# Gate cells, query prefetch, split loads and warm-up matmuls in a fused attention and MoE kernel

## The chip, the cores and the metric

The kernel runs on one core of a Trainium2 chip. A core has five engines that run side by side and meet through semaphores: PE (TensorE, matrix multiplication; PEld is its weight load), ACT (ScalarE, activation functions), DVE (VectorE, elementwise work), POOL (GpSimd, here for memsets and for issuing loads that cast) and SP (SyncE, here for issuing other transfers). The metric is the device time of one execution in microseconds (us). The kernel before took 968.65 us, the median of 11 runs (965.88 to 978.82).

## The reference

Four images of 384 by 32 pixels with 128 channels are attended. Keys and values are the same: the pixels averaged over 4 by 4 blocks (768 per image) and multiplied by `w_sr`. The attention's output is the input of a two-layer feed-forward net.

```python
kv_pool = kv.reshape(B, H // r, r, W // r, r, C).mean(axis=(2, 4))   # r = 4
kv_flat = kv_pool.reshape(B, -1, C) @ w_sr                           # keys and values
s = (1.0 / np.sqrt(C)) * (q @ kv_flat.transpose(0, 2, 1))
a = softmax(s)                                                       # over the 768 keys
x = (a @ kv_flat).reshape(B * N, C)                                  # 49152 rows
h = x @ w_in                                                         # d_ff = 2048
out = (h * sigmoid(1.702 * h)) @ w_out
```

## The kernel before

The 49152 query rows are cut into 96 groups of 512 (index i for attention, g for the feed-forward net, here called MoE), and four groups make a supergroup (index s, 24 of them). Keys of an image come in six chunks of 128 (index jc). The work has two halves of 48 groups: attention, then MoE, then attention, then MoE.

**Fills and drains.** A fill takes up to three (group, chunk) pairs: PE multiplies into half of six score banks of PSUM, and one activation of ScalarE (exponential in `fill_attn`, L324; gelu in `fill_moe`, L490) moves up to 128x1536 numbers to SBUF, to the tile `ag`. Fills alternate between two halves of three banks, so a fill p needs the activation of fill p - 2 to have ended. A drain multiplies what is in `ag` by the values (`drain_attn`, L333) or by `w_out` (`drain_moe`, L495), into two other banks, from which DVE evacuates. A planner written in Python, with its own running time `now`, its costs `COST` and its list `extras` of side jobs, decides at build time how PE's instructions of drains and side jobs stand between fills. Each engine then executes its instructions in that order.

**The start.** The keys of image 0 come from raw pixels that GpSimd loads in six chunks (`load_chunk`, L125); PE pools them with a small matrix (`pool_chunk`, L134), DVE copies the result to SBUF (L137), PE makes keys and values (`key_and_value`, L155 and L156) and DVE copies these (L157, L158). The first four supergroups of queries are loaded by GpSimd (L213) and transposed by PE (`transpose_q`, L224, copied out by DVE in L230). The table `first` (L567) gives the order in which this stands around the first 20 fills: ahead of fill 7 the transposes of group 7, ahead of fill 8 the pooling of chunk 2, and so on. `warm` (L276) puts matmuls whose result nobody reads among them.

**Pixels of image 1** are loaded the same way, and written over x tiles that are not yet in use, from group 13 on; from group 16 on PE pools a chunk per group and makes its keys a group later. Images 2 and 3 are added up by accumulating loads during the first MoE stage.

**Later queries** are cast to bf16 in DRAM by GpSimd (`cast_q`, L201), and from there loaded transposed by SP (`load_qT`, L206) into tiles of `qpool`.

**Gates.** `background(i)` runs when the planner reaches group i and issues such loads. GpSimd has little else to do and would issue everything at once; so ahead of a load stands `gate()` (L416 to L419): DVE writes the cell tile `gate_tile`, then GpSimd writes the same cells. The framework that sets the semaphores sees two writers of one place, so GpSimd waits until DVE has come as far as its write. The next gate writes the same cells again.

SP's queue is in order, too: the loads of queries, the writebacks of x (`put_away`, L405), the transposed reloads of x (`bring_back`, L411) and the output stores (L506).

Of the kernel before, what the change touches and what calls it, by code (L numbers as in the profile page):

```python
# [24 lines left out]
def kernel(  # L25
    ctx, tc, q, kv, w_sr, moe_w_in, moe_w_out, out,
):
    nc = tc.nc
# [5 lines left out]
    JC = J // 128  # L34
# [6 lines left out]
    NS = NG // 4  # L41
# [24 lines left out]
    kvsum = ctx.enter_context(tc.tile_pool(name="kvsum", bufs=1))  # L66
    kvres = ctx.enter_context(tc.tile_pool(name="kvres", bufs=2))
    kvtmp = ctx.enter_context(tc.tile_pool(name="kvtmp", bufs=1))
    qpool = ctx.enter_context(tc.tile_pool(name="qpool", bufs=3))
    agpool = ctx.enter_context(tc.tile_pool(name="ag", bufs=1))  # L70
    npool = ctx.enter_context(tc.tile_pool(name="norm", bufs=3))
    opool = ctx.enter_context(tc.tile_pool(name="op", bufs=3))
# [48 lines left out]
    def load_chunk(b, jc):  # L121

        a, ch = divmod(jc, HC)
        t = x_tile(XS - 1 - jc)
        nc.gpsimd.dma_start(out=t, in_=kv_r[b, a, ch])  # L125
        kv_tiles[b, jc] = t.rearrange("p (wp w1 c) -> p w1 wp c", w1=r, c=C)
# [34 lines left out]
    def add_kv(b, n):  # L161
        i, w = divmod(n, r)
        if n == 0:
            kv_sums[b] = kvsum.tile([Hp, 2, Wp, C], F32, name="kvs")
        for i2 in range(2):
            nc.gpsimd.dma_start(out=kv_sums[b][:, i2], in_=kv_p[b, i, w, :, i2],  # L166
                                **({"accum_op": ADD} if n else {}))
# [31 lines left out]
    def cast_q(s):  # L199
        sl = slice(s * SG, (s + 1) * SG)  # L200
        nc.gpsimd.dma_start(out=q_bf[sl, :].rearrange("(p i) c -> p (i c)", p=128),  # L201
                            in_=q_flat[sl, :].rearrange("(p i) c -> p (i c)", p=128))

    def load_qT(s):
        qTs[s] = qpool.tile([128, 1, SG], BF, name="qT")
        nc.sync.dma_start_transpose(out=qTs[s], in_=q_bf[s * SG:(s + 1) * SG, :])  # L206


    QS = 4
# [99 lines left out]
    early = range(NG // R, NG // R + EARLY)  # L309
# [92 lines left out]
    def put_away(n, m):  # L402
        o = m * PART
        lo = n * XS * SG + o * T
        nc.sync.dma_start(out=x_bf[lo:lo + PART * T, :].rearrange("(k p) c -> p k c", p=T),  # L405
                          in_=x[:, o * T:(o + PART) * T].rearrange("p (k c) -> p k c", k=PART))

    def bring_back(n, m):
        o = m * PART
        lo = n * XS * SG + o * T  # L410
        nc.sync.dma_start_transpose(out=x[:, o * T:(o + PART) * T].unsqueeze(1), in_=x_bf[lo:lo + PART * T, :])  # L411

    av_of = {}
    gate_tile = cpool.tile([1, 8], F32)

    def gate():  # L416

        nc.vector.memset(gate_tile, 0.0)  # L418
        nc.gpsimd.memset(gate_tile, 0.0)  # L419

    CAST = 5

    def background(i):

        s = i // 4
        if i % 4 == 0:
            if QS <= s + 2 < NS:
                load_qT(s + 2)
            if CAST <= s + CAST < NS:
                gate()  # L430
                cast_q(s + CAST)
        if i == 13:
            gate()
            for jc in range(JC):
                load_chunk(1, jc)
        if 0 <= i - 17 < JC:
            extras.append((key_and_value, 1, i - 17))
        if 0 <= i - 16 < JC:
            extras.append((pool_chunk, 1, i - 16))
        if i in (30, 34, 38):  # L440
            put_away(0, (i - 30) // 4)
        if i in (33, 37, 41):
            bring_back(0, (i - 33) // 4)
        if i == 26:
            gate()
            nc.gpsimd.dma_start(out=w_in_sb, in_=moe_w_in)
        if i == 34:
            gate()
            nc.gpsimd.dma_start(out=w_out_sb, in_=moe_w_out.rearrange("(o p) c -> p o c", p=128))

    def background_moe(g):

        n, g = divmod(g, 4 * XS)
        m, odd = divmod(g - 9, 2)
        m += FIRST
        if n == 0 and FIRST <= m < RT // PART:
            (bring_back if odd else put_away)(n, m)
        g += n * 4 * XS
        nonlocal low
        if g == 12:  # L460
            low = EARLY * JC
            order[:] = [f for f in order if f >= low // K]
        if g in (40, 46):
            i = early[0] + 4 * (g // 46)
            begun.add(("a", i))
            background(i)
        for b, lo in ((2, 2), (3, 24)):
            if lo <= g < lo + 8:
                gate()
                add_kv(b, g - lo)  # L470
            if g in (lo + 10, lo + 12):
                use_kv(b, (g - lo - 10) // 2)

    def use_kv(b, a):
        nonlocal extra_at
        sum_kv(b, a)
        on_dve(3.5)
        extra_at = max(extra_at, dve + 1.5)
        extras.extend([(transpose_pooled, b, a), (make_k, b, a), (make_v, b, a)])

    extras = []
# [59 lines left out]
    begun = set()  # L541
# [4 lines left out]
    def prepare(p):  # L546

        nonlocal now
        for f, *args in first.get(p, ()):
            if f in COST:  # L550
                now = max(now, free[next_acc()])
            f(*args)
            if f in COST:
                now += COST[f][0]
                free[last_acc] = now + COST[f][1]
        kind, part = seq[p]
        for i, jc in part:
            if (kind, i) not in begun:
                begun.add((kind, i))
                (background if kind == "a" else background_moe)(i)  # L560
            while kind == "a" and ((key_and_value, i // GB, jc) in extras or (transpose_q, i) in extras):
                f, *args = extras.pop(0)
                now = max(now, free[next_acc()]) + COST[f][0]
                f(*args)
                free[last_acc] = now + COST[f][1]

    first = {  # L567
        0: [(pool_chunk, 0, 0), (transpose_q, 0), (warm, 1), (key_chunk, 0, 0), (transpose_q, 1), (warm, 1)],
        1: [(value_chunk, 0, 0), (warm, 3)],
        2: [(pool_chunk, 0, 1), (warm, 2), (key_and_value, 0, 1), (warm, 1), (transpose_q, 2)],  # L570
        3: [(transpose_q, 3)],
        4: [(transpose_q, 4)],
# [52 lines left out]
    for n in range(len(seq)):  # L625
        fill(n + 2)
        while True:
# [33 lines left out]
            kind, i, c = source[0]  # L661
# [55 lines left out]
```

## Time and profile before

The profiled execution took 965.16 us, its span 963.4 us.

| engine | busy us | what it does most |
|---|---|---|
| ACT | 944.1 | 512 gelu activations (688.4 us), 189 exponentials (250.0 us) |
| PE | 949.0 | four groups of matmuls: L488 414.7, L495 413.7, L333 162.2, L322 151.1 us |
| DVE | 337.9 | evacuations and a share of the exponentials |
| POOL | 68.3 | issues of loads, 38 gates |

A line of the timeline has the start, the busy time, the engine, the source line, the operation, what it writes and reads with sizes, the count, and in brackets the idle time of the engine ahead of it with the engine that ended it. A row can merge several instructions of the same kind. PE's matmuls overlap and their ends are modelled, so its busy time is above the time in which it is needed.

### The profile page before, as it was taken

Reading aid. Unit: us, or ns where it says so; the run is one execution under the profiler, and the core shown is the slowest. Engines: PE = TensorE matmul, PEld = TensorE weight load, DVE = VectorE, ACT = ScalarE, POOL = GpSimd, SP = SyncE. Lnnn points to the kernel's source line nnn. Section 1 sums busy time; section 2 is a strip of 40 time slices with the busy share of each in tenths; the row PEclk is TensorE's granted clock in tenths of the full one; section 3 lists DMA queues with packets and bytes.
Section 4 is the critical chain, followed back from the end, with each engine's and each line's share of the span. In section 5 each row is a group of like instructions: output and inputs, shape, how many; then the busy total and the mean of one; then the engine's idle time right before and its main releaser. Section 6 shows DMA issues by size and latency. Waiting matters only on the chain.

```text
span 963.4 us, 15072 instructions
## 1 busy us (share of the span) xinstructions
PE 949.0 (99%) x6285; PEld 501.6 (52%) x6285; DVE 337.9 (35%) x721; ACT 944.1 (98%) x706; POOL 68.3 (7%) x117
## 2 busy tenths in 40 slices
PE   7899999999999999999999999999999999999997
PEld 3577777444444444444446777744444444444443
DVE  4444333111577877777613333310110101010010
ACT  4999999999999999999999999999999999999997
POOL 4020100330000332000000000000000000000000
PEclk9999999999999999999999999999999999999999
DMA  9799993999852799215449795472222222222222
GB/s 183 149 203 157 167 198 77 126 156 181 166 110 39 107 143 122 35 30 81 62 73 171 127 205 115 106 127 38 44 34 44 42 34 40 38 33 38 39 35 43
DMA packets 372804, 94.38 MB, mean 98 GB/s; under 512 B 346688, under 2 KB 370368, under 8 KB 372416
## 3 DMA queue, kind: packets, MB, share of 16 engines
q1 hardware_dynamic: 342512, 60.78, 37.3%
q0 software_dynamic: 29168, 32.51, 22.7%
q8 instruction: 49, 0.80, 0.4%
q10 hardware_dynamic: 1056, 0.13, 0.1%
q14 instruction: 19, 0.16, 0.1%
HBM read 52.49 MB, written 48.23 MB: 105 GB/s over the span
## 4 chain that ended last, share of the span: by engine, by line
ACT 93%; PE 5%; issue 1%; DMA 1%; DVE 0%; POOL 0%; POOLq 0%
ACT ag L490 71%; ACT ag L324 21%; PE banks L322 3%; PE banks L333 2%; DMA x<-in_q_dram 1%; PE banks L134 0%; ACT L490 0%; PE banks L224 0%; PE banks L276 0%; DVE qT L230 0%; ACT L324 0%; DVE x L345 0%; PE banks L495 0%; DVE o_sb L503 0%; POOL x L125 0%
## 5 line engine op out<-in xcount | busy, mean ns | idle before, releaser
L490 ACT ACTIVATE ag<-banks 128x1536 bf16<-128x1536 f32 x512 | 688.4, 1561 | 0.0
L488 PE MATMUL banks<-x,w_in_sb 128*128 128x512 bf16 x1536 | 414.7, 379 | 0.2
L495 PE MATMUL banks<-ag,w_out_sb 128*128 128x512 bf16 x1536 | 413.7, 379 | 0.5 <-ACT ag L490 0.5
L324 ACT ACTIVATE ag<-banks 128x1536 bf16<-128x1536 f32 (+2 forms) x189 | 250.0, 1444 | 6.6 <-PE banks L322 6.4
L495 PEld LDWEIGHTS <-w_out_sb 128*128 128x128 bf16 x1536 | 149.8, 98 | 180.4 <-issue 1.0
L488 PEld LDWEIGHTS <-w_in_sb 128*128 128x128 bf16 x1536 | 148.2, 98 | 179.0 <-issue 22.2
L503 DVE STREAM_TRANSPOSE o_sb<-banks 128x512 f32<-128x512 f32 x96 | 68.7, 716 | 398.8 <-PE banks L495 386.3
L333 PEld LDWEIGHTS <-ag 128*128 128x128 bf16 x2304 | 145.7, 98 | 42.8 <-issue 0.7
L333 PE MATMUL banks<-v,ag 128*128 128x129 bf16 x2304 | 162.2, 220 | 0.3 <-DVE v L158 0.3
L322 PE MATMUL banks<-qT,kT 128*128 128x512 bf16 x552 | 151.1, 381 | 5.9 <-ACT ag L324 3.3
L345 DVE TENSOR_TENSOR x<-banks,rec 128x384 bf16<-128x384 f32 x128 | 71.3, 557 | 4.4
L342 DVE RECIPROCAL rec<-banks 128x3 f32<-128x3 f32 x128 | 23.0, 180 | 138.0 <-PE banks L333 137.9
L390 DVE SCALAR_TENSOR_TENSOR ea<-ea,eb 128x512 f32<-128x512 f32 x96 | 65.9, 686 | 2.7
L322 PEld LDWEIGHTS <-kT 128*128 128x128 bf16 x552 | 47.3, 98 | 33.5 <-issue 5.8
L166 POOL DMA_DIRECT2D kvs<-in_kv_dram x32 | 40.6, 1319 | 30.9 <-DMA kvs<-in_kv_dram 28.6
L419 POOL MEMSET gate_tile<- 1x8 f32 x38 | 4.9, 129 | 434.6 <-DVE gate_tile L418 434.6
L379 DVE TENSOR_SCALAR ea<-banks 128x512 f32<-128x512 f32 x24 | 16.6, 691 | 28.0 <-PE banks L363 28.0
L392 DVE SCALAR_TENSOR_TENSOR ag<-ea,ee 128x512 bf16<-128x512 f32 x24 | 16.6, 691 | 0.8
L385 DVE SCALAR_TENSOR_TENSOR eb<-eb,ea 128x512 f32<-128x512 f32 x24 | 16.4, 685 | 0.7
L230 DVE COPY qT<-banks 128x512 bf16<-128x512 bf16 x15 | 10.2, 690 | 7.8 <-PE banks L224 7.8
L387 DVE TENSOR_SCALAR ea<-eb 128x512 f32<-128x512 f32 x24 | 10.6, 442 | 0.7
L201 POOL DMA_DIRECT2D q_bf<-in_q_dram x20 | 9.9, 496 | 7.6 <-DMA x<-in_kv_dram 6.1
(58 smaller groups left out, 126.7 us busy)
## 6 DMA issues: line engine op xcount, KB each, us to landing
out_dram<-o_sb SPq DMA_DIRECT2D x382, 64.0 KB, 2.0
x_bf<-x SPq DMA_DIRECT2D x16, 768.0 KB, 5.9
kvs<-in_kv_dram POOLq DMA_DIRECT2D x32, 384.0 KB, 6.7
q_bf<-in_q_dram POOLq DMA_DIRECT2D x20, 512.0 KB, 7.4
x<-in_kv_dram POOLq DMA_DIRECT2D x12, 512.0 KB, 12.1
x<-in_q_dram POOLq DMA_DIRECT2D x7, 256.0 KB, 15.2
w_in_sb<-in_moe_w_in_dram POOLq DMA_DIRECT2D x1, 512.0 KB, 5.3
w_out_sb<-in_moe_w_out_dram POOLq DMA_DIRECT2D x1, 512.0 KB, 10.9
```

What stands on the lines that cost most here:

```text
L166: nc.gpsimd.dma_start(out=kv_sums[b][:, i2], in_=kv_p[b, i, w, :, i2], **({"accum_op": ADD} if n else {}))
L322: nc.tensor.matmul(ps[:, k, :], kTs[i // GB][:, jc * 128:(jc + 1) * 128], rhs, start=True, stop=True)
L324: nc.scalar.activation(place([("a",) + c for c in chunks]), ps, AF.Exp, scale=scale)
L333: nc.tensor.matmul(av_of[u][:, k * (C + 1):(k + 1) * (C + 1)], weights(("a", i, jc))[:, o:o + T], vs[i // GB][:, jc, 0:C + 1], start=(jc = ...
L342: nc.vector.reciprocal(rec, ps[:, :, C])
L345: nc.vector.tensor_tensor(to, ps[:, :, 0:C], rec.unsqueeze(2).broadcast_to([128, TS, C]), MUL)
L379: nc.vector.tensor_scalar(a, ps, scale / LN2, -126.0, MUL, MAX)
L390: nc.vector.scalar_tensor_tensor(a, a, COEFFS[k], b, ADD, MUL)
L488: nc.tensor.matmul(ps[:, k, :], w_in_sb[:, fc * 128:(fc + 1) * 128], x[:, g % (4 * XS) * G:(g % (4 * XS) + 1) * G], start=True, stop=True)
L490: nc.scalar.activation(place([("m",) + c for c in chunks]), ps, AF.Gelu_apprx_sigmoid)
L495: nc.tensor.matmul(o_of[g], w_out_sb[:, fc, :], weights(("m", g, fc)), start=(fc == 0), stop=(fc == FCH - 1))
L503: nc.vector.transpose(o_sb, o_of.pop(g))
```

## The change

- A gate writes one of eight cells in turn, instead of all eight.
- `qpool` has four buffers instead of three, and transposed queries are loaded three supergroups ahead of the running one instead of two.
- The six loads of image 1's pixels are issued in two parts of three, at groups 10 and 13, each behind a gate. Its chunks are pooled one group sooner, from group 15 on, and the keys from group 16 on.
- In the first MoE stage, the background of group 48 alone is run ahead, at g = 40. That of group 52 is run when the second attention half reaches it.
- Of the warm-up matmuls in `first`, three are gone.

```diff
-    qpool = ctx.enter_context(tc.tile_pool(name="qpool", bufs=3))
+    qpool = ctx.enter_context(tc.tile_pool(name="qpool", bufs=4))
...
+    gates = [0]
+
     def gate():
 
-        nc.vector.memset(gate_tile, 0.0)
-        nc.gpsimd.memset(gate_tile, 0.0)
+        one = gate_tile[:, gates[0] % 8:gates[0] % 8 + 1]
+        gates[0] += 1
+        nc.vector.memset(one, 0.0)
+        nc.gpsimd.memset(one, 0.0)
...
         if i % 4 == 0:
-            if QS <= s + 2 < NS:
-                load_qT(s + 2)
+            if QS <= s + 3 < NS:
+                load_qT(s + 3)
...
-        if i == 13:
+        if i in (10, 13):
             gate()
-            for jc in range(JC):
+            for jc in range(i - 10, i - 7):
                 load_chunk(1, jc)
-        if 0 <= i - 17 < JC:
-            extras.append((key_and_value, 1, i - 17))
         if 0 <= i - 16 < JC:
-            extras.append((pool_chunk, 1, i - 16))
+            extras.append((key_and_value, 1, i - 16))
+        if 0 <= i - 15 < JC:
+            extras.append((pool_chunk, 1, i - 15))
...
-        if g in (40, 46):
-            i = early[0] + 4 * (g // 46)
-            begun.add(("a", i))
-            background(i)
+        if g == 40:
+            background(early[0])
...
-        0: [(pool_chunk, 0, 0), (transpose_q, 0), (warm, 1), (key_chunk, 0, 0), (transpose_q, 1), (warm, 1)],
-        1: [(value_chunk, 0, 0), (warm, 3)],
+        0: [(pool_chunk, 0, 0), (transpose_q, 0), (warm, 1), (key_chunk, 0, 0), (transpose_q, 1)],
+        1: [(value_chunk, 0, 0), (warm, 1)],
```

## The prediction

> **What bounds the kernel now.** I read the page's busy table first, then ScalarE's own waits, then its timeline at the start, then what DVE and GpSimd did in the same microseconds.
>
> ```profile
> span 963.4 us, 15072 instructions
> PE 949.0 (99%) x6285; PEld 501.6 (52%) x6285; DVE 337.9 (35%) x721; ACT 944.1 (98%) x706; POOL 68.3 (7%) x117
> ACT 93%; PE 5%; issue 1%; DMA 1%; DVE 0%; POOL 0%; POOLq 0%
> ```
>
> ScalarE (ACT) is busy for 944.1 of 963.4 us and carries 93% of the chain that ended last. PE shows 99%, but matmul ends are modelled; only 5% of the chain is PE's. None of ScalarE's 702 activations and copies, nor its four table loads, is touched by the diff. So the change can only move ScalarE's idle time: 963.4 - 944.1 = 19.3 us. Where that lies is in ScalarE's timeline of the first 160 us (the last column is idle time ahead, and what ended it):
>
> ```profile
> 7.91 0.58 ACT L228 COPY qT<-banks 128x512 bf16<-128x512 bf16 x1 [5.88 <-PE banks L224]
> 9.61 0.60 ACT L324 ACTIVATE ag<-banks 128x512 bf16<-128x512 f32 x1 [1.11 <-PE banks L322]
> 10.74 0.60 ACT L324 ACTIVATE ag<-banks 128x512 bf16<-128x512 f32 x1 [0.53 <-PE banks L322]
> 13.06 4.73 ACT L324 ACTIVATE ag<-banks 128x1024 bf16<-128x1024 f32 x5 [1.72 <-PE banks L322]
> 19.43 1.02 ACT L324 ACTIVATE ag<-banks 128x1024 bf16<-128x1024 f32 x1 [1.65 <-PE banks L322]
> 20.71 1.02 ACT L324 ACTIVATE ag<-banks 128x1024 bf16<-128x1024 f32 x1 [0.26 <-PE banks L322]
> 22.56 55.67 ACT L324 ACTIVATE ag<-banks 128x1536 bf16<-128x1536 f32 x42 [0.82 <-PE banks L322]
> 78.57 67.70 ACT L324 ACTIVATE ag<-banks 128x1536 bf16<-128x1536 f32 x50 [0.34 <-PE banks L322]
> ```
>
> About 10 us lie ahead of 13.06 (with 0.75 before the first table load), 2.73 between 17.79 and 22.56, 0.5 between 22.56 and 78.57, and the last 6.0 us are the drain after the final activation at 957.4. After 78.57 ScalarE never waits: the second half of attention and both MoE stages have nothing to give. Only 2.73 us are near the edited lines. Why does ScalarE wait there? DVE's timeline in that stretch:
>
> ```profile
> 14.24 1.44 DVE L230 COPY qT<-banks 128x512 bf16<-128x512 bf16 x2 [0.27 <-PE banks L224]
> 17.80 0.68 DVE L230 COPY qT<-banks 128x512 bf16<-128x512 bf16 x1 [2.13 <-PE banks L224]
> 17.81 0.07 DVE L418 MEMSET gate_tile<- 1x8 f32 x1
> ```
>
> and GpSimd's (POOL):
>
> ```profile
> 14.68 0.70 POOL L213 DMA_DIRECT2D x<-in_q_dram  x1 [0.57 <-DMA x<-in_q_dram]
> 17.15 0.52 POOL L201 DMA_DIRECT2D q_bf<-in_q_dram  x1 [1.77 <-DMA x<-in_kv_dram]
> 17.66 0.09 POOL L419 MEMSET gate_tile<- 1x8 f32 x1
> ```
>
> DVE sat idle for 2.13 us before copying query group 6 out of PSUM. The profile blames PE's transpose, but PE started that at 15.52 for 0.39 us, so it had long been done. In program order the second gate's DVE memset stands directly ahead of this copy; in the program before it waits for GpSimd, since it overwrites the cell that GpSimd's memset of the first gate writes. GpSimd reached that memset at 17.66, after a cast that itself waited for a landing load. DVE starts within 0.1 us of its end. So a pacing gate, meant to hold GpSimd, held DVE, then PE (matmuls of group 6 at 18.54), then ScalarE. A second cost rides on it: of three stretches of the trace, the granted clock is below 1.00 in the middle one alone.
>
> ```profile
> 13.06:17.80 4.74, 3.39 (x28) 1.92 (x25) 2.30 (x4) 4.73 (x5) 2.02 (x4) 1.00 1.11 216
> 17.80:22.56 4.76, 3.63 (x33) 1.76 (x34) 2.06 (x6) 2.05 (x2) 0.59 (x2) 0.64 1.12 213
> 22.56:36.00 13.44, 10.10 (x106) 5.75 (x102) 5.13 (x14) 13.44 (x11) 0.49 (x1) 1.00 1.08 213
> ```
>
> The columns are length, busy time of PE, PEld, DVE, ACT and POOL, granted clock, DMA share, GB/s. PE idles for 1.7 us, then runs at a mean clock of 0.64, which produces the waits of 0.26 and part of 0.82.
>
> **What the Trainium skill says.** "TensorE: Matmul & The Clock Gate", section "Architectural detail", says that ScalarE's and DVE's queues are strict first-in-first-out: a waiting memset holds every later copy. The trace agrees: 2.13 us. The same page, "What's actually happening", puts PE's clock at half after an idle window of some 3.4 us, and back at full after a busy one. The trace agrees in kind, not in size: 1.7 us of idle sufficed here, and about 4.7 us passed before full speed. "DMA: Bandwidth & Descriptors", section "Issuing engines are not separate DMA queues", says that loads issued by SP and GpSimd share the same 16 engines; the DMA share of 1.08 to 1.14 above, with both queues active from 36 us on, fits.
>
> **The change part by part.**
>
> *Gates in eight cells.* The memsets stay (38 on each engine, one more after; 65 and 94 ns); in the built program the DVE one waits for nothing at first use, while GpSimd's still waits for its own gate's DVE memset. Follow the fills of the score banks (p7 is query group 6, p8 group 7, p9 to p11 pooled chunk 2). Before, ScalarE began p7, p8, p9 and p10 at 19.43, 20.71, 22.56 and 23.90 (22.56 + 1.34). After:
> - group 6's copy starts 0.44 after its transpose (as 12.19 to 12.63): 15.52 + 0.44 = 15.96, and ends at 16.64. Group 7: 16.44 + 0.44 = 16.88 to 17.56.
> - p7's matmuls need the bank that ScalarE leaves at 13.06 + 4 x 0.946 = 16.84, so they run at 16.9 to 17.4; p7 is ready before p6 ends at 17.79. Wait 1.65 becomes 0; p8 follows at 18.74, wait 0.26 becomes 0.
> - chunk 2's pooling: its load had landed by 17.15 (the cast that reuses its semaphore was issued then), so it starts at 17.4; copy to SBUF at +0.59, done +0.88 = 18.3; key matmul 18.4; key copy +0.31 to +0.60 = 19.0; p9's three matmuls to ScalarE 0.85 (77.72 to 78.57): p9 at 19.9.
> - what is late next: chunk 3. It had landed only by 20.26 (the next cast's issue). Pooling 20.3, p10's matmuls 0.40 later, ScalarE 0.85 later: p10 at 21.55, against p9's end at 21.24.
> Gain at p10: 23.90 - 21.55 = 2.35 us. Chunk 4 landed by 22.67 and is then wanted at 23.7, so it holds nothing. Chunk 5 is wanted at 29.52 - 2.35 = 27.2; the landings at 17.1, 20.2 and 22.6 with half a chunk of queries between put it near 26.5, an estimate; if it is late the gain falls by some tenths. Ends: 1.5 (chunks late) to 2.73 (all three waits gone). I take 2.35.
>
> *Three warm-up matmuls fewer* (0.21 us each by their start spacing, 0.64 in all, between 8.9 and 10.3). They bring the first two activations forward by some 0.2 and 0.5 us, but 13.06 follows from pooling chunk 1 at 10.62, which waited for its load (landed by 10.86, next issue). Worth 0. Hidden only while PE keeps its clock. If it drops to half near 12 us, each step of two score matmuls and four transposes costs 2 x 0.43 + 4 x 0.11 = 1.3 us against ScalarE's 0.946, over four steps 1.4 us lost. Bounds 0 and -1.4; I take 0, since 13 stay at the start and five between 7.8 and 12.1.
>
> *Queries three supergroups ahead, four buffers.* In the built program the load of supergroup 4 gets a fresh buffer, so SP may issue it when its cast has landed, about 32.4 (SP's wait for it was 31.2 us from 1.2), not at 35.75; each later one comes some 10.7 us (four groups at 2 x 1.337) sooner. No ScalarE wait in the trace names a query load, so 0 gained. SP stands first in line for the same buffer release as before, so the writebacks and out stores queued behind it are not later. In the MoE stage one load of two moves to the start of the second attention half; with ScalarE idle 0.03 us there, 0.
>
> *Second pixels in two parts, one group sooner.* Three loads leave two groups (2 x 2.67 us) ahead of the gate at 48.42, minus 2.35: 40.7. Pooling begins one group earlier: 58.97 - 2.67 - 2.35 = 53.9. So they have 13 us; before, the first had under 7.9 (51.26 to 58.97) and PE did not wait. The same 96 pooling matmuls and twelve small ones are moved, none added. In 36 to 79 us PE is busy 42.47 of 43.00, so placement may change the two ScalarE waits of 0.13 and 0.34: between -0.5 and +0.7, I take 0. One gate more: 0.16 us on engines with room.
>
> **Sum.** -2.35 + 0 + 0 + 0 = -2.35 us on the profiled execution's 965.16 (span 963.4, 1.8 around it): 962.8. The eleven plain times have a median of 968.65, 3.5 above it; the same subtraction there gives 966.3 us, -0.24%. Half a per cent, 4.84 us, is about what a measurement of this kernel can tell from no change.
>
> **Rivals.**
> - *More than the gate's own stall.* Plain executions take 3.5 us more than the profiled one. If that is late loads at the start, lengthening GpSimd's way to its gate with DVE held meanwhile, the edit returns both: 968.65 - 5.85 = 962.8, faster by 0.6%. For: the spread of 965.9 to 978.8. Against: late loads also delay the pooling, which no gate causes.
> - *The clock drops for want of warm-up.* 966.3 + 1.4 = 967.7. For: one 1.7 us gap was enough. Against: the gaps opened here are about 0.2 to 0.5 us.
> - *The change doesn't do what it says*: DVE was held by something the records miss (a few matmul records can be missing), or chunks 2 to 4 take the wait over. Then 968.6. Against: the 0.1 us between GpSimd's memset and DVE's.
> - *Slower: second pixels not landed.* PE works in order, so pooling at 53.9 stops the score matmuls where it has almost no slack. Two full banks cover 2.7 us. It eats the gain when a load takes 13.2 + 2.7 + 2.35 = 18.2 us, and costs 0.5% at 23: 973.5 or more. For: landing medians of 12.1 and 15.2 us on the page for the first loads, and the query transposes now sharing this stretch. Against: DMA share 0.66 in 40 to 60.
>
> **How the numbers follow.** Forecast 0.62 (its own range 965.3 to 967.6), more than the stall 0.15, clock 0.10, no effect 0.06, slower 0.07. Faster by over 0.5%: 0.16; within: 0.77 (0.62 + 0.10 + 0.06, rounded with the first rival); slower: 0.07. The range 962.5 to 969.4 takes in all but the slower case and the tail of the first rival.
>
> **What would show it.** Right: no idle of 1.65 before an activation near 17.8, DVE copying group 6 near 16 us, clock 1.00 from 17.8 to 22.6, ScalarE's long run starting near 19.9 to 21.6, ScalarE idle of about 17 us in all. Wrong: pooling that waits for a load near 54 us; a clock under 1 between 10 and 16 us; an idle ScalarE anywhere after 80 us; the last activation ending elsewhere than near 955.

## The result, and the profile after

The changed kernel took 963.32 us in the median (12 executions, from 962.83), the kernel before 969.68 (47 executions); the ratio is 0.9932, 95% interval 0.9899 to 0.9965. A second comparison on one chip gave 963.14 against 966.36, ratio 0.9951 (0.9929 to 0.9974). The forecast was 966.3 us, -0.24%. Its full range, 962.5 to 969.4, holds the result, the range of its main case, 965.3 to 967.6, does not; and the gain is two to three times as large, so part of its source was not in my sum.

The ratios here and below leave out executions more than 1.5% above the fastest of their kernel, four of these 12 and five of the 47; with them the mean is 973.4 us against 971.2, so it is the usual execution that became faster, while a faster average is not shown.

The profile on record is of one of those four, 1000.31 us. A second profiled execution of the changed kernel took 962.96 us. Its page, and ScalarE's timeline at the start:

```profile
span 961.1 us, 14956 instructions
PE 940.6 (98%) x6168; PEld 500.8 (52%) x6282; DVE 338.4 (35%) x722; ACT 944.0 (98%) x706; POOL 68.1 (7%) x118
...
9.01 0.60 ACT L324 ACTIVATE ag<-banks 128x512 bf16<-128x512 f32 x1 [0.69 <-PE banks L322]
10.03 0.60 ACT L324 ACTIVATE ag<-banks 128x512 bf16<-128x512 f32 x1 [0.42 <-PE banks L322]
12.87 6.57 ACT L324 ACTIVATE ag<-banks 128x1024 bf16<-128x1024 f32 x7 [2.25 <-PE banks L224]
19.62 1.45 ACT L324 ACTIVATE ag<-banks 128x1536 bf16<-128x1536 f32 x1 [0.18 <-PE banks L322]
21.81 121.98 ACT L324 ACTIVATE ag<-banks 128x1536 bf16<-128x1536 f32 x91 [0.73 <-PE banks L322]
```

Five two-bank activations, followed by two that waited, have become one run of seven. ScalarE's idle time is 961.1 - 944.0 = 17.1 us (19.3 before). DVE's timeline shows why, and the windows the clock (the columns as before):

```profile
15.43 0.06 DVE L422 MEMSET gate_tile<- 1x1 f32 x1
15.76 0.69 DVE L230 COPY qT<-banks 128x512 bf16<-128x512 bf16 x1 [0.27 <-PE banks L224]
16.68 0.69 DVE L230 COPY qT<-banks 128x512 bf16<-128x512 bf16 x1 [0.22 <-PE banks L224]
```

```profile
13.06:17.80 4.74, 4.26 (x43) 2.76 (x44) 3.54 (x8) 4.74 (x6) 2.01 (x4) 1.00 1.11 217
17.80:22.56 4.76, 3.11 (x29) 1.42 (x29) 1.52 (x6) 3.84 (x4) 0.58 (x2) 1.00 1.10 209
```

The gate's memset waits for nothing; ahead of group 6's copy DVE is idle for 0.27 us, not 2.13.

The execution of 1000.31 us has the same start (copies at 15.94 and 16.85, the first three-bank activation at 19.80). What it adds is in ScalarE's timeline, and in PE's:

```profile
19.80 35.41 ACT L324 ACTIVATE ag<-banks 128x1536 bf16<-128x1536 f32 x27 [0.18 <-PE banks L322]
82.22 1.45 ACT L324 ACTIVATE ag<-banks 128x1536 bf16<-128x1536 f32 x1 [27.01 <-PE banks L322]
84.44 9.74 ACT L324 ACTIVATE ag<-banks 128x1536 bf16<-128x1536 f32 x7 [0.78 <-PE banks L322]
103.27 1.45 ACT L324 ACTIVATE ag<-banks 128x1536 bf16<-128x1536 f32 x1 [9.09 <-PE banks L322]
```

```profile
52.91 0.81 PE L322 MATMUL banks<-qT,kT 128*128 128x512 bf16 x3
79.97 0.61 PE L134 MATMUL banks<-sum,x 128*128 128x32 bf16 x16 [26.25 <-DMA x<-in_kv_dram]
```

PE reached the pooling of image 1 at 53.7 and stood still for its first chunk until 79.97: the mechanism and the place of my slower rival. What PE waited for before ScalarE's second long wait, ahead of 103.27, the profile does not name.

### The profile page after: what moved, and what is told of

It is laid out like the page before. It is cut to its first block, busy times and chain, and to the rows that moved or that the text cites. A ratio compares the mean times of both kernels' runs of the same rounds, so it can differ in the third digit from the quotient of the medians.

```text
span 998.4 us, 15070 instructions
## 1 busy us (share of the span) xinstructions
PE 950.8 (95%) x6282; PEld 502.8 (50%) x6282; DVE 338.3 (34%) x722; ACT 944.3 (95%) x706; POOL 68.1 (7%) x118
## 4 chain that ended last, share of the span: by engine, by line
ACT 60%; PE 32%; DMA 5%; issue 2%; DVE 0%; POOL 0%; POOLq 0%
ACT ag L492 51%; PE banks L497 9%; ACT ag L324 9%; PE banks L490 9%; PE banks L333 7%; PE banks L322 7%; DMA x<-in_kv_dram 5%; PE banks L134 0%; ACT L492 0%; PE banks L363 0%; POOL x L213 0%; PE banks L276 0%; DVE o_sb L505 0%; DVE qT L230 0%; POOL x L125 0%
## 5 line engine op out<-in xcount | busy, mean ns | idle before, releaser
L423 POOL MEMSET gate_tile<- 1x1 f32 x39 | 4.8, 123 | 468.3 <-DVE gate_tile L422 468.3
L134 PE MATMUL banks<-sum,x 128*128 128x32 bf16 x192 | 6.8, 179 | 27.4 <-DMA x<-in_kv_dram 27.4
L134 PEld LDWEIGHTS <-x 128*128 128x128 bf16 x192 | 6.5, 98 | 31.4 <-DMA x<-in_kv_dram 29.0
L137 DVE CAST pTc<-banks 128x128 bf16<-128x128 f32 x12 | 3.5, 291 | 39.7 <-PE banks L134 39.7
```

## The experiments

The comparisons were made on three chips, each kernel with the kernel before on its own chip. "Long" below counts the executions above 966 us among all of a kernel.

| kernel | median, its before | ratio (95%) | long | long, its before |
|---|---|---|---|---|
| changed, second comparison | 963.14, 966.36 | 0.9951 (0.9929-0.9974) | 4 of 22 | 28 of 53 |
| changed, two ahead again | 978.29, 966.36 | 1.0048 (1.0011-1.0085) | 14 of 16 | 28 of 53 |
| changed, loads together again | 963.28, 966.36 | 0.9967 (0.9950-0.9985) | 2 of 22 | 28 of 53 |
| before + gates | 968.87, 969.12 | 0.9971 (0.9943-1.0000) | 15 of 22 | 27 of 43 |
| before + three ahead | 964.46, 969.12 | 0.9949 (0.9926-0.9972) | 4 of 22 | 27 of 43 |
| before - casts 8 to 11 | 964.50, 968.62 | 0.9948 (0.9925-0.9970) | 2 of 20 | 51 of 61 |
| before - image 1's loads | 964.77, 968.62 | 0.9941 (0.9916-0.9966) | 2 of 20 | 51 of 61 |
| loads at group 8 | 968.33, 968.62 | 0.9972 (0.9947-0.9998) | 15 of 22 | 51 of 61 |
| loads together, repeated | 964.09, 968.62 | 0.9946 (0.9897-0.9996) | 5 of 12 | 51 of 61 |

The kernel before has its shortest executions at 964 to 965 us, but half or more of all lie above 966, up to 977 and beyond. My forecast rested on one execution of 965.16.

**The changed kernel again** (no edit).

> The changed kernel once more, to see what its usual execution looks like beside the one already profiled, in which PE waited 26 us for image 1's first chunk. If the gates alone made the gain, as forecast: ScalarE's idle time near 17 us, the span near 961, and no wait after 22.6 us. If the loads of image 1 are the cost to be watched: in some executions PE stops at pooling near 54 us for 10 us or more, and these take 985 us or more.

Measured: idle 17.1 us, span 961.1, and no wait longer than 0.22 us after 22.6, as the gates' share of the forecast has it. Eighteen of 22 executions lie between 962.9 and 963.4, one at 967.9, three at 990.8 to 993.6. Both halves of the expectation hold.

**Two supergroups ahead again.**

```diff
-    qpool = ctx.enter_context(tc.tile_pool(name="qpool", bufs=4))
+    qpool = ctx.enter_context(tc.tile_pool(name="qpool", bufs=3))
...
-            if QS <= s + 3 < NS:
-                load_qT(s + 3)
+            if QS <= s + 2 < NS:
+                load_qT(s + 2)
...
-        if g == 40:
-            background(early[0])
+        if g in (40, 46):
+            i = early[0] + 4 * (g // 46)
+            begun.add(("a", i))
+            background(i)
```

> The changed kernel with queries loaded two supergroups ahead from three buffers again, as before; gates, split loads and fewer warm-ups stay. Theory A (the long wait for image 1's chunk comes from a transposed query load that now runs in the same microseconds as image 1's loads): the wait is gone in every execution, all near 963. Theory B (the wait comes from issuing image 1's loads at group 10 and pooling them a group sooner): executions of 985 us and more are as frequent as in the changed kernel, about one in three.

Both theories fail. No execution is near 963 (the shortest took 965.14), and none of 16 reaches 985. PE's waits in the profiled one (981.74 us) name another tensor:

```profile
PE banks L322 <- DMA qT<-q_bf: 15.9, 2, 13.3
PE banks L322 <- ACT ag L324: 3.2, 6, 1.0
PE banks L134 <- DMA x<-in_kv_dram: 2.5, 4, 1.1
```

(total, times, longest.) PE waits 13.3 us at once for transposed queries. With two ahead it is the query load that comes late, and more often than in the kernel before (14 of 16 long, against 28 of 53). Whether the gates or the split loads make it so was not separated.

**Image 1's loads together again.**

```diff
-        if i in (10, 13):
+        if i == 13:
             gate()
-            for jc in range(i - 10, i - 7):
+            for jc in range(JC):
                 load_chunk(1, jc)
-        if 0 <= i - 16 < JC:
-            extras.append((key_and_value, 1, i - 16))
-        if 0 <= i - 15 < JC:
-            extras.append((pool_chunk, 1, i - 15))
+        if 0 <= i - 17 < JC:
+            extras.append((key_and_value, 1, i - 17))
+        if 0 <= i - 16 < JC:
+            extras.append((pool_chunk, 1, i - 16))
```

> The changed kernel with image 1's six loads issued together at group 13 and pooled from group 16 again; gates, three supergroups ahead and fewer warm-ups stay. Theory A: the loads still meet a query transpose, so executions of 985 us stay or become more frequent. Theory B: they are gone, all near 963 to 966. If the gain beyond 2.35 us came from the earlier loads, the fastest executions stay near 963 but the middle of the times moves up by some 3 us, as in the kernel before.

The usual time is unchanged, 963.28: the split of the loads gives nothing in it. The profiled execution (979.48 us) still has PE wait 14.6 us for image 1's chunk, so that wait can come without the split. Neither theory fits in full: no execution reaches 985, but two are long. The repeat:

> Once more the changed kernel with image 1's loads together at group 13, pooled from group 16; two of its 22 executions took more than 964 us, against four of 22 of the changed kernel. If that is a real difference: at most three of this run's lie above 966, and the usual time is 963.2 again. If it was chance: four to eight.

Five of 12 above 966, up to 987.67: by its own terms the low count of the first time was chance. Over both, 7 of 34 are long, against 8 of 34 of the changed kernel; above 980 us lie 1 and 7 (two more of the loads together at 979.5 and 979.8). Whether the split makes the long wait longer stays open.

**The kernel before, three more profiled executions.** Theory C, put in full with the gates below: what the changed kernel gained beyond the start comes from queries that no longer arrive late.

> The kernel before, a second look. Its times reach from 964 to 986 us. If the start alone varies (my first rival): ScalarE's idle time between 13 and 23 us is longer than 2.73 us by what the execution is longer than 965. If image 1's loads vary: ScalarE waits between 55 and 80 us by that much. If neither: 965 us and the waits of the first look.

The first, 965.27 us, shows the waits already known ("neither").

> The kernel before once more, for an execution above 967 us if it comes. Theory C: by what it is above 965, PE waits for a transposed query load (qT) between 55 and 110 us. Rivals: it waits for image 1's chunks there, or the start up to 23 us is longer.

> As the look before it: theory C says that whatever the execution takes above 965 us is PE waiting for qT between 55 and 110 us; the rivals say image 1's chunks, or the start.

These came at 973.94 and 975.52 us. In the first of the two, PE, then ScalarE:

```profile
78.40 0.84 PE L333 MATMUL banks<-v,ag 128*128 128x129 bf16 x12
86.59 1.46 PE L322 MATMUL banks<-qT,kT 128*128 128x512 bf16 x3 [7.34 <-DMA qT<-q_bf]
```

```profile
77.28 2.79 ACT L324 ACTIVATE ag<-banks 128x1536 bf16<-128x1536 f32 x2 [0.34 <-PE banks L322]
88.09 1.45 ACT L324 ACTIVATE ag<-banks 128x1536 bf16<-128x1536 f32 x1 [8.02 <-PE banks L322]
90.18 20.47 ACT L324 ACTIVATE ag<-banks 128x1536 bf16<-128x1536 f32 x15 [0.64 <-PE banks L322]
```

and PE's waits in the second:

```profile
PE banks L322 <- DMA qT<-q_bf: 8.7, 1, 8.7
```

Theory C holds for both: the extra is PE waiting for qT near 80 us, where the first group of supergroup 6 is due. ScalarE loses 8.0 and 9.4 us there at once, and 1.4 and 1.6 in short waits soon after. PE's clock did not fall at the start in these two, so they are to be compared with the shortest executions, 964.1 us, which they exceed by 9.8 and 11.4. The load of supergroup 6 was issued at 56.59 and landed 30.0 us later. In the profile that I forecast from it was issued at 57.89, and the view of that line says

```profile
DMA to landing us min/median/max: 21.9/21.9/21.9
```

that is 79.8 us. In the 973.94 us execution the load holds up the third fill after ScalarE's run of 42. In the profile of the forecast that fill is

```profile
80.38 0.81 PE L322 MATMUL banks<-qT,kT 128*128 128x512 bf16 x3
```

The margin was 0.6 us, and no wait showed.

**The gates alone, and three supergroups ahead alone.** The edits are those hunks of the diff, on the kernel before.

> The kernel before with the eight gate cells alone. Theory C (the gates give the whole start-up gain and nothing else; what else the changed kernel gained comes from queries arriving three supergroups ahead): the shortest times fall by 2.1 us, from 965.1 to 963.0, and the longer ones stay as spread out as in the kernel before, to some 975; ratio near 0.998. Rival (the gates also caused the spread of the kernel before, by holding DVE at later gates): all times within 1 us of 963.

> The kernel before with the queries three supergroups ahead (four buffers) alone. Theory C: the usual time stays at 965.1, since the start is untouched, but far fewer executions lie above 966.5 than the half of the kernel before; the ratio is near 0.998 or lower. Rival (query loads were never late): ratio 1.000 and the same spread as before.

With the gates, the shortest executions fall to 962.65 (964.13 before, the same chip); the rest are at least as spread as before, 15 of 22 above 966, three above 980 (one of 43 before) and the longest at 1008.71, more than the 975 expected. So executions above 980 need neither the split nor the queries three ahead. The interval reaches 1.0, so the median shows no sure gain. With three ahead, 18 of 22 lie between 963.8 and 965.4, and the ratio, 0.9949, is about that of the whole change in its second comparison. The profiled execution shows how: supergroup 6's load was issued at 45.69, ahead of image 1's loads, and landed in 4.0 us. Now supergroup 7's load, issued at 56.5, takes 22.1 us, but it is wanted some 10.7 us after supergroup 6's, near 90 by that estimate. Theory C holds in kind. One number was wrong: the usual time is not 965.1. Eleven executions lie at 963.8 to 964.1, others at 964.9 to 965.4. The profiled one, 963.83, is of the first kind, and PE's clock did not fall in it, although DVE was held as before.

**What makes the query load late?** Two kernels leave work out of the kernel before.

```diff
     def cast_q(s):
+        if 8 <= s < 12:
+            return
...
-        nc.sync.dma_start_transpose(out=qTs[s], in_=q_bf[s * SG:(s + 1) * SG, :])
+        nc.sync.dma_start_transpose(out=qTs[s], in_=q_bf[(s - 4 if 8 <= s < 12 else s) * SG:(s - 3 if 8 <= s < 12 else s + 1) * SG, :])
```

> The kernel before without the casts of query supergroups 8 to 11, which GpSimd issues from 48 to 81 us (their loads read the cast rows of supergroups 4 to 7 again, so this work is left out). Theory D (the late query load shares the DMA engines with these casts): executions above 967 us, nearly half of the kernel before, become rare, and supergroup 6's load lands well before 78 us. Theory E (it shares them with image 1's pixel loads): the share of long executions stays near a half.

```diff
-        nc.gpsimd.dma_start(out=t, in_=kv_r[b, a, ch])
+        if b == 0:
+            nc.gpsimd.dma_start(out=t, in_=kv_r[b, a, ch])
```

> The kernel before without image 1's six pixel loads (its keys are made from image 0's pixels still in the tiles, so this work is left out). Theory E: no execution above 966, query supergroup 6, whose load is issued near 57 us, lands within 10 us. Theory D: the share of executions above 967 us stays near a half.

Each theory expected the other kernel to change nothing, and each was wrong in that: long executions all but vanish in both, 2 of 20 against 51 of 61. Supergroup 6's load lands in 15.6 us without the casts and 7.0 us without image 1's loads. So neither is enough by itself. How the queues share the 16 DMA engines stands in the view of DMA (q0 is GpSimd's queue, q1 SP's with the transposes; packets, MB, and the time of the packets as a share of 16 engines). From 60 to 65 us, then from 70 to 75, in the 973.94 us execution of the kernel before:

```profile
q0 software_dynamic: 272, 0.99, 97.6%
q1 hardware_dynamic: 240, 0.06, 8.8%
...
q1 hardware_dynamic: 503, 0.13, 92.2%
q0 software_dynamic: 24, 0.17, 19.2%
```

From 70 to 75 us in its execution of 965.16 us, then in the changed kernel's of 1000.31 us, while PE stood still:

```profile
q0 software_dynamic: 60, 0.88, 114.8%
q1 hardware_dynamic: 1563, 0.40, 50.7%
...
q1 hardware_dynamic: 291, 0.07, 146.9%
q0 software_dynamic: 18, 0.07, 11.9%
```

There are two delays. While image 1's pixels land (the last at 71.0), GpSimd's queue fills the engines and the transpose hardly moves; from 60 to 65 us that is so in the 965.16 us execution too (99.3% and 6.4%). After that the transposes' own packets are slow, with few of GpSimd's beside them. Five microseconds of 16 engines are 80 us, so a packet took 0.922 x 80 / 503 = 147 ns in the long execution, 26 ns in the usual one and 404 ns in the changed kernel's. What slows them was not found.

**Image 1's loads at group 8.**

```diff
         s = i // 4
+        if i == 8:
+            gate()
+            for jc in range(JC):
+                load_chunk(1, jc)
```

(on the changed kernel with loads together; the loads at group 13 go.)

> Gates, three supergroups ahead and fewer warm-ups, with image 1's six loads issued together at group 8, ahead of that group's cast, and pooled from group 16 as before: some 25 us between issue and use instead of 8. If a long way from issue to use is enough: all executions near 963 and none above 966, a version better than both. If the loads then meet the query transposes of supergroups 4 and 5 at 33 to 45 us: long executions stay, as in the changed kernel, by waits for image 1's chunks or for supergroup 5's queries.

The second branch came in part: 15 of 22 executions are long, most at 968.1 to 969.4. The profiled one, 963.72, was not among them, so what these wait for was not seen. It is no better version, and I found none that surely is: loads together have the same usual time as the changed kernel, and three ahead alone gives up the gates' 1 us but has more even times (two of 22 above 968; the mean of all is 965.5 us, that of the changed kernel 967.2, on another chip).

## Why the prediction was right, and where it was not

The result lies in the full range in part by luck. The sum had 2.35 us where the median fell by 6.4; the range reached that far down for a rival that put the rest in the wrong place, and a gain above half a per cent had a chance of 0.16.

*The gates.* Right, step by step. Forecast, and measured in the execution on record: group 6's copy 15.96, 15.94; group 7's 16.88, 16.85; p7's matmuls 16.9, 16.92; pooling of chunk 2 17.4, 17.35; p9 19.9, 19.80. In the execution of 962.96 us, what comes late next is chunk 3, as forecast: p10 at 21.81 with a wait of 0.73 (forecast 21.55). In the one on record chunk 3 was in time. Up to the table load that opens MoE the gain is 146.10 to 143.80, 2.3 us, between two executions with the same first 7.7 us (965.27 and 962.96); the forecast was 2.35. It is a gain against executions in which the clock fell. Where it did not fall, with DVE held all the same, MoE began at 144.93 (three ahead alone), and the gates are worth 1.1. So the second cost that I put in the same sum is some 1.2 us, but comes only in some executions: three of the seven profiled ones in which DVE was held.

*Warm-up matmuls.* Right at 0, by the traces; not run alone. The first activations moved to 9.01 and 10.03, the third stayed (12.87, and 12.85 in the kernel before at 965.27 us). The clock stayed at 1.00, so the clock rival fell.

*Three supergroups ahead.* This is the step that failed: "No ScalarE wait in the trace names a query load, so 0 gained." It was true of that execution. But half or more of the executions of the kernel before are long, the two long ones that were profiled wait for a query load, 7.3 and 8.7 us on PE, and the lever that removes the wait is the part I put at nothing. Measured alone, it is worth 969.12 - 964.46 = 4.7 us in the median. With the gates' 1.1 to 2.3 that makes 5.8 to 7.0; the first comparison gave 6.4 us, the second 3.2, on a chip where fewer executions of the kernel before were long. Also, I subtracted 2.35 from a median that stood 3.5 us above the execution I had read, and asked where those 3.5 us lay only in a rival.

*That rival* (more than the gate's own stall, 962.8) had the time right and the place wrong. The start varies by about one us, with the clock. The rest lay near 80 us in the profiled executions, not at GpSimd's way to its gate.

*The slower rival* named the right mechanism. Image 1's chunks landed 39.4 us or more after issue in the execution on record, against the 18.2 us from which it eats the gain; ScalarE lost 27.0 us, and 9.1 more later. I gave it 0.07. Seven of the changed kernel's 34 executions lie above 980 us. In the second comparison the mean over all 22 executions is 967.2, against 967.8 before; in the first it was the higher one. "Against: DMA share 0.66 in 40 to 60" failed as an argument: it is the share of the kernel before, and the change moves loads into that stretch, where the share is 1.0 in the execution on record.

*Split loads.* 0 in the usual time, as forecast.

Settled: which waits go, and by which part. Shown too: long executions of the kernel before become rare without the casts, and without image 1's loads. Argued only: that the changed kernel's long wait for image 1 has the same source, as the transposes' packets are slow in both. Open: what makes these packets slow in one execution and not in the next.

## What to carry to other kernels

A load that nobody waits for in the profile may still be on time by less than a microsecond: compare issue time plus landing time with the moment of first use, for each stream of loads. When the median of the plain times is above the profiled execution's by more than the effect looked for, profile again until the longer kind is caught, before costing an edit at zero. A pacing gate made of two writers of one cell paces both; give each gate its own cell if only one engine is to be held.

## What was unexpected of the hardware

"DMA: Bandwidth & Descriptors", section "Issuing engines are not separate DMA queues", in the Trainium skill says that loads of SP and GpSimd run on the same 16 engines and interleave. The DMA shares shown in the forecast say nothing of this: they are of stretches up to 36 us, and from 8 to 35.7 us only GpSimd's loads were under way. The stretch from 60 to 65 us agrees with it, 97.6% for GpSimd's queue and 8.8% for SP's, and shows how uneven the shares can be: the transpose moved 0.06 MB of its 0.52. That its packets can then take 147 or 404 ns instead of 26, with few of GpSimd's packets beside them, was not expected.

PE's clock fell in three of the seven profiled executions in which DVE was held, after the same idle gap of 1.7 us. Where it fell, it was at half for 3.41 us; the 4.7 us of my forecast was the length of the window that I had asked for. In the first profile:

```profile
15.35:18.76 3.41, 1.59 (x13) 0.87 (x12) 1.28 (x4) 2.44 (x3) 0.63 (x3) 1.00 1.05 213
18.76:22.17 3.41, 3.02 (x25) 1.37 (x24) 1.10 (x4) 2.05 (x2) 0.59 (x2) 0.50 1.09 205
```

In each trace the changes of the clock lie whole numbers of 3.41 us apart. Laid out in such steps, the gap falls into one step in the three executions whose clock fell (PE busy for 1.6 to 1.7 us of it), and is divided between two in the four whose clock stayed (1.9 us or more in each). That fits all seven; it was not tested.
